# Rows of x, two modulation tables and the row statistics placed at other steps of the first two batches

## The chip, the cores and the metric

The kernel runs on one core of a Trainium2 chip. Its engines are TensorE (PE in the profile, with its weight loads as PEld), VectorE (DVE), ScalarE (ACT), GpSimd (POOL) and SyncE (SP, which here only issues transfers). Each engine works through its own list of instructions in order and waits on semaphores for the others. Transfers run on 16 DMA engines; they are issued by SP or, for a few early ones, by POOL. The metric is device time in microseconds (us) of the core, as the median of several executions.

## The reference

An adaptive layer norm with six modulation vectors, an S4D convolution (a long convolution whose kernel is a sum of 256 damped oscillations for each channel), and a token-mixing MLP:

```python
mod = (_silu(c) @ w_mod).reshape(c.shape[0], 6, 1, -1)
sa, ca, ga, sb, cb, gb = (mod[:, 0], mod[:, 1], mod[:, 2], mod[:, 3], mod[:, 4], mod[:, 5])
h = _layernorm(x, axis=-1) * (1 + ca) + sa
x = x + ga * _A_ref(h, A_log_A_real, A_A_imag, A_C_real, A_C_imag, A_log_dt, A_D_skip)
h = _layernorm(x, axis=-1) * (1 + cb) + sb
x = x + gb * _B_ref(h, B_w1, B_b1, B_w2, B_b2)
```

```python
# _A_ref
A = -jnp.exp(log_A_real) + 1j * A_imag
C = (C_real + 1j * C_imag) * dt[:, None]
P = jnp.exp((A * dt[:, None])[:, :, None] * pos[None, None, :])
K = 2.0 * jnp.einsum("dn,dnl->dl", C, P).real
y = jnp.fft.irfft(Uf * Kf[None, :, :], L2)[:, :, :L]      # Uf, Kf: rfft of u and K
# _B_ref
h = _layernorm(x, axis=-1)
u = _gelu(jnp.einsum("bsd,sf->bdf", h, w1) + b1)
y = jnp.einsum("bdf,fs->bds", u, w2) + b2
```

There are 2048 tokens, 448 channels, 256 oscillations for a channel and 1792 hidden units. Everything is float32. `shift` in this document is `sa`, the vector `mod[0]`; `mod[1]` is the scale and `mod[2]` the gate of the convolution.

## The kernel before

The program has two parts. The first, up to about 384 us, builds the convolution kernel of all channels, transforms x and the kernel, multiplies and transforms back. The second, from there to the end, is the MLP on PE. The change lies in the first 130 us of the first part.

**Steps, batches and windows.** The 448 channels are 28 groups of 16, and each group is done in two halves of 128 oscillations: 56 steps, in batches of 8. A batch opens with `window(s)` (s = 0, 8, 16, ...), in which the exponentials of its eight steps are made, and goes on with its eight steps, in which sines and cosines are made; so ACT changes its table of functions twice in a batch.

- `st_exponents(s)` (PE): parameter rows `lex` times the table `tab`, into `xe`, `xg`. `st_exp(s)` (ACT): their exponentials `mag`. `st_mag2(s)` (POOL, L654 and L656): a product `m` of them.
- `st_phase(s)` (PE): rows `lph` times `tab`, into `xe`, `xg`. `st_abs` and `st_step` (ACT, L664 to L677): sines and cosines. From these POOL makes `G` (L679, L680) and DVE makes `E` (L681 to L687), which PE multiplies in `st_kgen` (L710) two steps later. `E` and `G` have three buffers each.
- `st_s1` (PE, L748) is the first transform of the finished kernel of two groups, on alternate steps from step 8 on; its results are copied by ACT, or in the last step of a batch by DVE (L755).

**The path of x.** x stands in `xt` as 16 rows of 128 x 448 (a row here is one position r of every 16 tokens). `x_load(r0, n, G)` issues the transfers of n rows as four transfers on POOL's queue. `u_stats(r)` (DVE, L527 and L528) takes mean and variance of a row. At the start of window 8 `logs(True)` on ACT and `u_scale` on DVE turn all 16 pairs into `rs` and `nm`, so that none of it starts before the last row's statistics are there; `u_norm` (POOL for rows 0 to 5, ACT later, L543 and L541) normalises. `u_rows(r)` (PE, L553) transforms a row into two `pu` tiles, DVE multiplies these by `mod[1]` into `yt` (L556), and SP stores `yt`. Rows 0 to 4 and 5 go in window 8, one row in each of the steps 9 to 14, the last four in window 16. The tables `late_rows` (step to rows) and, in window 0, the line for rows 0 to 3 say where the statistics are taken; `between()`, which runs behind E's four operations in the steps up to 15, takes them and then goes on with the parameters of the next channels (`more`, L399 to L450).

**Modulation vectors.** `wm_load(k, place)` loads the 448 x 448 block of `w_mod` for vector k (784 KB). `modulation(k, halves)` (PE, L489) multiplies it in two halves into one `pm` tile, which ACT copies to `mod[k]` (L493) at the next `flush(act)`. `mod_steps` says in which steps; vector 0 has its two halves at e = 2 and e = 4 of window 8. In step 9 DVE multiplies `mod[0]` by `mod[2]` (L1103). `mod[0]` is first read in batch 24. The dictionary `late` says in which step each block is issued and to where; blocks 0 and 2 go to free room and on POOL's queue, block 1 to free room on SP's, block 3 over rows 0 to 3 of `xt`, which have been transformed by then.

**Queues and buffers.** The order on PE, ACT, DVE and POOL is that of the code. SP's is that of the code up to step 7; from step 8 on it is set by the scheduler. `pu`, `pm` and the results of `st_s1` share three PSUM buffers (`pms`, tag `ms`); a `pu` pair takes two.

Of the kernel before, what the change touches and what calls it, by code (L numbers as in the profile page):

```python
# [221 lines left out]
def tile_adaln_s4d_mixer(ctx, tc, i, out):  # L222
    nc = tc.nc
# [20 lines left out]
    with ExitStack() as es:  # L244
# [47 lines left out]
        PP = 112  # L292
# [35 lines left out]
        def wm_load(k, tile, eng=nc.sync):  # L328
            wms[k] = tile
            eng.dma_start(wms[k], i["w_mod"][:, k * D : (k + 1) * D].rearrange("(q p) d -> p q d", p=PP))  # L330
# [11 lines left out]
        def wm_slot(k):  # L342
            w = wm0.rearrange("p k d -> p (k d)")[0:PP]
            return w[:, 4 * D * (k % 4) : 4 * D * (k % 4 + 1)].rearrange("p (q d) -> p q d", q=4)
# [2 lines left out]

        late = {
            2: lambda: wm_load(2, wm_slot(2), G),
            3: lambda: wm_load(0, wm_slot(0), G),  # L350
            6: lambda: [
                nc.sync.dma_start(wu, i["WU"]),
                nc.sync.dma_start(wc, i["WC"].rearrange("p (c m) -> p c m", c=2)),
            ],
            9: lambda: [nc.sync.dma_start(svt, i["SV"]), wm_load(3, xt[0:PP, 0:4])],
            10: lambda: [s2_load(0), s2_load(1)],
            11: lambda: [s2_load(2), s2_load(3)],
        }


# [204 lines left out]
        def s2_load(n):  # L565
            s2s[n] = sp2.tile([P, 2, P], F32, tag="s2", name="s2", bufs=4)
            nc.sync.dma_start(s2s[n], s2_v[:, 2 * n : 2 * n + 2])
# [290 lines left out]
        def first_chain():  # L858
# [7 lines left out]
            def split(eng, src):  # L866

                hl = room.pop()
                eng.tensor_copy(hl[:, 0].bitcast(F32R), src)
                eng.tensor_tensor(hl[:, 1].bitcast(F32R), src, hl[:, 0], ALU.subtract)  # L870
                return hl
# [66 lines left out]
            tt(xa, xa, u, ALU.subtract)  # L938
            store(ha, (0, 1), (1, 1))
            hl = split(G, p64)  # L940
            direct(hl, lph, 64, 0)
            hc = split(V, xa)
            direct(hc, lph, 96, 0)
# [59 lines left out]
        def window(s):  # L1003
            angle()
            logs(s == 8)
            if s == 8:
                u_scale()
                u_norm(0)
                u_norm(1)

            if s == 0:
                st_exponents(s)
            for e in range(BATCH):
                st_exp(s + e)

                if e + 1 < BATCH:
                    st_exponents(s + e + 1)
                else:
                    st_phase(s)
                mellow()  # L1020
                if s == 8 and e == 0:
                    tt(mod[1], mod[1], mod[2], ALU.mult)
                flush(dve)
                flush(act)
                flush(late_act)
                if s < 32:
                    more(WPACE[s // 8][e])
                if s == 0 and e >= 4:
                    u_stats(e - 4)
                if s and e < (2 if s <= 32 else 1):  # L1030
                    st_kgen(s - (2 if s <= 32 else 1) + e)
                elif e == (7 if s == 32 else 5):
                    if s == 8:
                        yks[0] = y0.tile([P, 32, DC], F32, tag="yk", name="yk0")
                    st_s1(s > 16)

                if s == 8 and e in (2, 4):
                    modulation(0, e // 4)
                if s in (8, 16):
                    some(u_rows, rows, (1, 1, 1, 1, 1, 0, 0, 1)[e])  # L1040
                elif s == 24 and e != 5:
                    some(u_cols, cols, 1)

                if s == 32 and e == 2:
                    nc.sync.dma_start(t0, i["T0"].rearrange("p (j m) -> p j m", j=2))
                if s == 32 and e == 5:
                    pc_load(1)
                if s >= 40 and e == 2:
                    piece(False)
                if s >= 32 and e == 4:  # L1050
                    piece(pieces[0] < NP, V)
                if s == 0 and e in (4, 5):
                    st_mag2(e - 4)
                elif s and (e < 2 or s >= 32):
                    st_mag2(s + e)
                if s == 8 and e == 0:
                    u_norm(e + 2)
                if s == 0 and e == 3:
                    for r in range(4):
                        dsk_copy(r)  # L1060
            if s == 0:

                S.activation(one, one, AF.Sin)
# [2 lines left out]

        WPACE = [[0] * 8, [0, 2, 3, 4, 5, 5, 5, 5], [0, 5, 4, 4, 4, 4, 4, 4], [2] * 8]
        pace = [2] * 32
        mod_steps = {2: (1, 0), 3: (1, 1), 6: (2, 0, 1)}
        late_rows = {3: (4, 5), 4: (6, 7), 5: (8, 9), 6: (10, 11), 7: (12, 13, 14, 15)}  # L1070
        tail = NHALF + 3
        for s in range(tail):
            if s == 32:
# [25 lines left out]

            def between():  # L1100
                flush(dve)
                if s == 9:
                    tt(mod[0], mod[0], mod[2], ALU.mult)  # L1103
                for r in late_rows.get(s, ()):
                    u_stats(r)
                if s < len(pace):
                    more(pace[s])
# [36 lines left out]
                st_kgen(s - 1)  # L1144


            if s < 2:
                x_load(4 + 4 * s, 4 + 4 * s, G)
            free = s > 7 and not st_s1(s % BATCH == BATCH - 1)
            if s + 2 < 32 and (s + 2) % BATCH > 1:  # L1150
                st_mag2(s + 2)
# [324 lines left out]
```

## Time and profile before

| | us |
|---|---|
| median of 3 executions | 690.65 |
| these executions | 687.97, 690.65, 694.99 |
| the profiled execution, its own time | 685.43 |
| its span in the profile | 683.7 |

The rest of the profiled execution's time, 1.73 us, lies outside the span.

| engine | busy us | share of the span |
|---|---|---|
| PE | 612.7 | 90% |
| DVE | 452.6 | 66% |
| ACT | 439.0 | 64% |
| POOL | 268.1 | 39% |

These shares are means over two very different parts. From about 384 us on PE is busy nearly all the time and all else waits for it. Before that PE, DVE, ACT and POOL take turns, and what a change there is worth has to be read from the timeline of that place. A row of the timeline gives start, duration, engine, source line, operation, the tiles written and read, how many instructions are merged (a matmul of float32 shows as several), and in square brackets how long the engine had been idle and what ended that. POOL's queue carries 8 transfers of 224 KB and 4 of 448 KB for x and 2 of 784 KB for `w_mod` in this profile.

### The profile page before, as it was taken

The page shows a single profiled execution, that of the slowest core. Times are in us where ns is not written, and L with a number is a line of the kernel's source. Part 1 is how long each engine was busy: PE and PEld are TensorE (multiplying, and loading weights), DVE is VectorE, ACT ScalarE, POOL GpSimd, SP SyncE. Part 2 cuts the span into 40 slices and gives each one's busy share as a digit, 9 for nine tenths or more (in the row PEclk, how much of TensorE's full clock was granted, in tenths as well). Part 3 has the DMA queues.
Part 4 walks back from the last instruction along what each step waited for, and adds up shares of the span by engine and source line. Part 5 has one row for each costly group of instructions (what it writes and reads, how often), then busy time and mean ns, then how long its engine had stood idle before and what let it go on. Part 6 is the DMA issues. An engine that isn't in the chain of part 4 may idle for free. (4 is left out here: it accounts for less than half of the span.)

```text
span 683.7 us, 18263 instructions
## 1 busy us (share of the span) xinstructions
PE 612.7 (90%) x7180; PEld 456.0 (67%) x7180; DVE 452.6 (66%) x870; ACT 439.0 (64%) x880; POOL 268.1 (39%) x323
## 2 busy tenths in 40 slices
PE   0786778879989899989989899999999999999997
PEld 0443345535535556565657677779999999999996
DVE  7498799888779596895967587777422454433331
ACT  5967597988988999999945588877322322222220
POOL 6397457448458889789847100000000000000000
PEclk9989888999999999999999999999999999999999
DMA  7695563377896857344359799956674355555530
GB/s 176 199 201 111 181 200 120 128 269 223 251 310 190 234 116 216 97 133 136 97 140 315 237 256 255 239 128 199 160 221 135 95 142 168 165 161 170 167 119 28
DMA packets 105923, 121.14 MB, mean 177 GB/s; under 512 B 13098, under 2 KB 94286, under 8 KB 105710
## 3 DMA queue, kind: packets, MB, share of 16 engines
q1 hardware_dynamic: 104478, 113.92, 58.1%
q0 software_dynamic: 1360, 6.06, 4.1%
q8 instruction: 57, 0.93, 0.6%
q14 instruction: 28, 0.23, 0.1%
HBM read 84.59 MB, written 34.87 MB: 175 GB/s over the span
## 5 line engine op out<-in xcount | busy, mean ns | idle before, releaser
L207 ACT CAST whi<-w 128x896 fp32r<-128x896 f32 x64 | 59.8, 940 | 132.2 <-PE o L1443 84.5
L679 POOL TENSOR_TENSOR G<-mag,gs 128x512 f32<-128x512 f32 x56 | 71.8, 1281 | 66.1 <-ACT gs L675 65.9
L216 DVE TENSOR_TENSOR wlo<-w,whi 128x896 fp32r<-128x896 f32 x64 | 68.0, 1086 | 40.3 <-ACT whi L207 27.9
L1373 PE MATMUL acc<-h3h,whi 128*128 128x448 f32 x224 | 83.3, 372 | 1.6 <-ACT h3h L1278 1.6
L1374 PE MATMUL acc<-h3l,whi 128*128 128x448 f32 x224 | 82.1, 367 | 0.1
L1443 PE MATMUL o<-ul,whi 128*128 128x448 f32 x224 | 81.3, 363 | 0.0
L1375 PE MATMUL acc<-h3h,wlo 128*128 128x448 f32 x224 | 81.2, 362 | 0.0
L1442 PE MATMUL o<-uh,whi 128*128 128x448 f32 x224 | 81.2, 362 | 0.0
L1444 PE MATMUL o<-uh,wlo 128*128 128x448 f32 x224 | 80.6, 360 | 0.0
L710 PEld LDWEIGHTS kg<-E,G 128*32 128x32 f32 x3584 | 57.3, 116 | 34.9 <-issue 14.5
L627 PE MATMUL xg<-tab,lph 64*128 64x512 f32 x112 | 62.9, 563 | 12.4 <-DVE E L687 4.7
L710 PE MATMUL kg<-E,G 128*32 128x64 f32 x3584 | 67.1, 230 | 7.0 <-issue 3.3
L680 POOL TENSOR_TENSOR G<-mag,gs 128x512 f32<-128x512 f32 x56 | 71.8, 1282 | 0.0
L627 PE MATMUL xe<-tab,lph 64*128 64x512 f32 x112 | 63.5, 569 | 4.7 <-ACT gs L676 2.6
L1446 DVE SCALAR_TENSOR_TENSOR y<-o,b,mod 128x448 f32<-128x448 f32 x16 | 10.9, 684 | 80.2 <-PE o L1444 80.2
L656 POOL TENSOR_TENSOR m<-mag,w 128x512 f32<-128x512 f32 x56 | 58.9, 1052 | 4.4
L681 DVE TENSOR_TENSOR E<-m,xe 128x512 f32<-128x512 f32 x56 | 38.1, 681 | 23.2 <-ACT xe L674 19.8
L1373 PEld LDWEIGHTS acc<-h3h,whi 128*128 128x128 f32 x224 | 42.4, 189 | 14.6 <-ACT h L1283 5.6
L627 PE MATMUL xe<-tab,lex 64*128 64x512 f32 x56 | 30.9, 569 | 19.2 <-DMA lex<-wm 17.0
L1375 PEld LDWEIGHTS acc<-h3h,wlo 128*128 128x128 f32 x224 | 42.3, 189 | 3.0
L1442 PEld LDWEIGHTS o<-uh,whi 128*128 128x128 f32 x224 | 42.0, 188 | 3.4
L1374 PEld LDWEIGHTS acc<-h3l,whi 128*128 128x128 f32 x224 | 42.4, 190 | 2.7 <-DVE h3l L1281 0.5
(239 smaller groups left out, 1440.1 us busy)
## 6 DMA issues: line engine op xcount, KB each, us to landing
w<-in_B_w_dram SPq DMA_DIRECT2D x64, 224.0 KB
w<-in_B_w_dram SPq DMA_DIRECT2D x32, 448.0 KB
yu_d<-yt SPq DMA_DIRECT2D x16, 448.0 KB
yi<-yu_d SPq DMA_DIRECT2D x16, 448.0 KB
us_d<-uo SPq DMA_DIRECT2D x16, 448.0 KB
u<-us_d SPq DMA_DIRECT2D x32, 224.0 KB
v_d<-vt SPq DMA_DIRECT2D x32, 224.0 KB
vt<-v_d SPq DMA_DIRECT2D x14, 448.0 KB
```

The source lines that it names most:

```text
L207: self.nc.scalar.copy(hi, w)
L216: eng.tensor_tensor(lo, w, hi.bitcast(F32), ALU.subtract)
L627: T.matmul(out[k], lhs[r], rhs[r], start=start, stop=stop)
L679: G.tensor_tensor(Gt[:, 1], mg_, v32(sg), ALU.mult)
L680: G.tensor_tensor(Gt[:, 0], mg_, v32(cg_), ALU.mult)
L710: T.matmul(kgs[g][32 * q : 32 * q + 32, m], Gt[:, c, d], E[:, c, d], start=h == 0 and c == 0 and m == 0, stop=h == 1 and c == 1, skip_grou ...
L1373: nc.tensor.matmul(acc[f], hi[:, fs], h3h[:, r], start=r == 0, stop=False)
L1374: nc.tensor.matmul(acc[f], hi[:, fs], h3l[:, r], start=False, stop=False)
L1375: nc.tensor.matmul(acc[f], lo[:, fs], h3h[:, r], start=False, stop=r == 15)
L1442: nc.tensor.matmul(o, hi[:, ks], uh[kh][:, k], start=kh == 0 and k == 0, stop=False)
L1443: nc.tensor.matmul(o, hi[:, ks], ul[kh][:, k], start=False, stop=False)
L1444: nc.tensor.matmul(o, lo[:, ks], uh[kh][:, k], start=False, stop=kh == 1 and k == 6)
```

## The change

```diff
         late = {
             2: lambda: wm_load(2, wm_slot(2), G),
-            3: lambda: wm_load(0, wm_slot(0), G),
             6: lambda: [
...
-            9: lambda: [nc.sync.dma_start(svt, i["SV"]), wm_load(3, xt[0:PP, 0:4])],
+            9: lambda: [nc.sync.dma_start(svt, i["SV"]), wm_load(0, xt[0:PP, 0:4])],
             10: lambda: [s2_load(0), s2_load(1)],
             11: lambda: [s2_load(2), s2_load(3)],
+            12: lambda: wm_load(3, xt[0:PP, 4:8]),
         }
...
             hl = split(G, p64)
+            x_load(4, 4, G)
             direct(hl, lph, 64, 0)
...
-                if s == 8 and e in (2, 4):
-                    modulation(0, e // 4)
...
-        mod_steps = {2: (1, 0), 3: (1, 1), 6: (2, 0, 1)}
-        late_rows = {3: (4, 5), 4: (6, 7), 5: (8, 9), 6: (10, 11), 7: (12, 13, 14, 15)}
+        mod_steps = {2: (1, 0), 3: (1, 1), 6: (2, 0, 1), 12: (0, 0), 13: (0, 1)}
+        late_rows = {0: (4, 5), 3: (6, 7), 5: (8, 9, 10), 6: (11, 12, 13), 7: (14, 15)}
...
-                if s == 9:
+                if s == 15:
                     tt(mod[0], mod[0], mod[2], ALU.mult)
...
-            if s < 2:
-                x_load(4 + 4 * s, 4 + 4 * s, G)
+            if s == 0:
+                x_load(8, 8, G)
```

Rows 4 to 7 of x are issued among the first parameters, before window 0, instead of behind step 0; rows 8 to 15 behind step 0 instead of behind step 1. The block of `w_mod` for vector 0 is no longer loaded by POOL in step 3 but by SP from step 9 on, over rows 0 to 3 of `xt`; the block for vector 3 goes over rows 4 to 7, from step 12 on. The two halves of modulation 0 move from window 8 to the ends of the steps 12 and 13, its copy by ACT with them, and the product with `mod[2]` from step 9 to step 15. The statistics of the rows 4 and 5 move from step 3 to step 0, 6 and 7 from 4 to 3, 10 from 6 to 5, 12 and 13 from 7 to 6. No arithmetic is added or left out.

POOL's list, from behind the split of the first parameters to step 2, before (`xt` rows of 1792 elements are the four transfers of rows 4 to 7, those of 3584 the rows 8 to 15, L654 and L656 are `st_mag2`):

```order
L477 COPY dsk<-dskr 1x112 x4
L654 TENSOR_TENSOR w<-mag 128x16
L656 TENSOR_TENSOR m_325<-mag,w 128x512
L654 TENSOR_TENSOR w<-mag 128x16
L656 TENSOR_TENSOR m_339<-mag,w 128x512
L679 TENSOR_TENSOR G<-mag,gs 128x512
L680 TENSOR_TENSOR G<-mag,gs 128x512
L305 DMA xt<-in_A_u_dram 32x1792 x4
L654 TENSOR_TENSOR w<-mag 128x16
L656 TENSOR_TENSOR m_415<-mag,w 128x512
L679 TENSOR_TENSOR G<-mag,gs 128x512
L680 TENSOR_TENSOR G<-mag,gs 128x512
```

and now:

```order
L305 DMA xt<-in_A_u_dram 32x1792 x4
L477 COPY dsk<-dskr 1x112 x4
L654 TENSOR_TENSOR w<-mag 128x16
L656 TENSOR_TENSOR m_329<-mag,w 128x512
L654 TENSOR_TENSOR w<-mag 128x16
L656 TENSOR_TENSOR m_343<-mag,w 128x512
L679 TENSOR_TENSOR G<-mag,gs 128x512
L680 TENSOR_TENSOR G<-mag,gs 128x512
L305 DMA xt<-in_A_u_dram 32x3584 x4
L654 TENSOR_TENSOR w<-mag 128x16
L656 TENSOR_TENSOR m_425<-mag,w 128x512
L679 TENSOR_TENSOR G<-mag,gs 128x512
```

Four issues have moved from between step 0 and step 1 to ahead of window 0; the four of rows 8 to 15 stand in their old place, and nothing stands behind step 1 in theirs.

DVE's list in step 0, before (`E`, then two operations on the next parameters):

```order
L681 TENSOR_TENSOR E<-m_325,xe 128x16x32
L682 SCALAR_TENSOR_TENSOR E<-mag,xe 128x16x32
L686 TENSOR_TENSOR E<-mag,xg 128x16x32
L687 TENSOR_TENSOR E<-m_325,xg 128x16x32
L399 SCALAR_TENSOR_TENSOR s<-xa,ya 128x256
L401 TENSOR_TENSOR ya<-ya,xa 128x256
```

and now:

```order
L681 TENSOR_TENSOR E<-m_329,xe 128x16x32
L682 SCALAR_TENSOR_TENSOR E<-mag,xe 128x16x32
L686 TENSOR_TENSOR E<-mag,xg 128x16x32
L687 TENSOR_TENSOR E<-m_329,xg 128x16x32
L527 BN_STATS st<-xt 128x6
L528 BN_AGGR mv<-st 128x2
L527 BN_STATS st<-xt 128x6
L528 BN_AGGR mv<-st 128x2
L399 SCALAR_TENSOR_TENSOR s<-xa,ya 128x256
L401 TENSOR_TENSOR ya<-ya,xa 128x256
```

The statistics of rows 4 and 5 now stand between E of step 0 and the parameters; step 7 has two rows behind E where it had four.

PE's list at the end of step 12, the last two matmuls of `st_phase(13)`, the row's transform and step 13's `st_kgen`, before:

```order
L627 MATMUL xe<-tab,lph_143 128x512
L627 MATMUL xg<-tab,lph_143 128x512
L553 MATMUL pu<-xt,wu 128x448 x2
L710 MATMUL kg<-E,G 32x64 x32
L627 MATMUL xe<-tab,lph_144 128x512
```

and now:

```order
L627 MATMUL xe<-tab,lph_143 128x512
L627 MATMUL xg<-tab,lph_143 128x512
L489 MATMUL pm<-xt,scb 128x448 x2
L553 MATMUL pu<-xt,wu 128x448 x2
L710 MATMUL kg<-E,G 32x64 x32
L627 MATMUL xe<-tab,lph_144 128x512
```

Half of modulation 0 stands ahead of the row's transform, and so ahead of all that PE does behind it; the same holds one step later for the other half.

## The prediction

> **What bounds the kernel now.** I read the chain of work that ended last, then the busy times by stretch, then the timeline of each engine up to 150 us. The chain is printed only back to about 384 us, where the MLP begins; from there on PE is the bound and the change touches nothing. First its line by engine, then three stretches, for which each engine's busy time, the granted clock of PE, the DMA engines' busy share and GB/s are given: steps 0 to 2 of batch 1, window 8, and the steps 8 to 15:
>
> ```profile
> PE 42%; ACT 1%; DVE 1%; issue 0%; ACTq 0%
> ...
> core 0: us, PE busy (x) PEld busy (x) DVE busy (x) ACT busy (x) POOL busy (x), PEclk, DMA share, GB/s
> 29.50:45.00 15.50, 11.55 (x158) 6.48 (x159) 15.13 (x18) 11.02 (x23) 14.74 (x20) 0.78 0.92 204
> ...
> 71.50:92.60 21.10, 18.80 (x252) 10.46 (x252) 16.04 (x40) 14.40 (x28) 7.18 (x10) 0.88 0.67 231
> 92.60:127.30 34.70, 27.68 (x531) 17.20 (x523) 34.30 (x54) 31.01 (x61) 28.52 (x28) 0.85 0.35 121
> ```
>
> The first is carried by DVE (15.13 of 15.50) and POOL (14.74) with the DMA engines nearly full (0.92), window 8 by PE (18.80 of 21.10), steps 8 to 15 by DVE (34.30 of 34.70). The end of batch 1 is read from DVE's timeline, with the two engines that wait for it behind:
>
> ```profile
> 41.83 3.44 DVE L410 SCALAR_TENSOR_TENSOR s<-t,s 128x256 f32<-128x256 f32 x1
> ...
> 47.59 0.61 DVE L527 BATCH_NORM_STATS2 st<-xt 128x6 f32<-128x448 f32 x1
> ...
> 49.07 0.69 DVE L681 TENSOR_TENSOR E<-m,xe 128x512 f32<-128x512 f32 x1
> ...
> 57.75 0.63 DVE L527 BATCH_NORM_STATS2 st<-xt 128x6 f32<-128x448 f32 x1 [1.60 <-DMA xt<-in_A_u_dram]
> ...
> 69.55 0.18 DVE L528 BATCH_NORM_AGGREGATE mv<-st 128x2 f32<-128x6 f32 x1
> ```
>
> ```profile
> 69.77 0.31 ACT L462 ACTIVATE rs<-mv,small_t 128x16 f32<-128x16 f32 x1 [2.36 <-DVE mv L528]
> ...
> 71.47 3.10 POOL L543 TENSOR_SCALAR xt<-xt,rs,nm 128x448 f32<-128x448 f32 x4 [7.35 <-DVE nm L536]
> ```
>
> DVE ends batch 1 with the last statistics; ACT has waited 2.36 us for them and POOL 7.35 us. Between 45.27 (the end of L410) and 69.73 DVE pauses once, 1.60 us, for rows 8 and 9 of x. So batch 1 is as long as DVE's list.
>
> **Part by part, batch 1.** POOL's rows:
>
> ```profile
> 30.01 1.28 POOL L679 TENSOR_TENSOR G<-mag,gs 128x512 f32<-128x512 f32 x1 [8.49 <-ACT gs L675]
> ...
> 32.46 2.00 POOL L305 DMA_DIRECT2D xt<-in_A_u_dram  x4
> ...
> 43.70 1.28 POOL L680 TENSOR_TENSOR G<-mag,gs 128x512 f32<-128x512 f32 x1
> ...
> 46.44 0.74 POOL L330 DMA_DIRECT2D wm<-in_w_mod_dram  x1
> ```
>
> ```profile
> DMA to landing us min/median/max: 3.9/10.0/17.9
> ```
>
> 1. *Rows 8 to 15.* The issue stands where that of rows 4 to 7 stood, 32.46 to 34.46. The slowest of the x transfers landed after 17.9 us, so they are there by 52.4. DVE asks for row 8 where E of step 5 ended, 57.75 - 1.60 = 56.15, less what it gains before (2.3 us, terms 2 and 3): 53.8. The wait goes: -1.60, with 1.4 us to spare; 784 KB of block 0 and the rows 4 to 7 have also left that stretch. Ends: 0 and -1.60.
>
> 2. *Statistics.* A pair takes 49.07 - 47.59 = 1.48. Steps 3 to 7 had six pairs and have five: -1.48. The pair in step 0 falls on a busy DVE (15.13 of 15.50) and pushes everything up to L410 back by 1.48.
>
> 3. *L410.* It took 3.44, and ended 0.3 after POOL's pair L679, L680 of step 2 (43.70 + 1.28 = 44.98): DVE was held, not working. POOL's pair comes 2.00 earlier, since four issues have left its unbroken run (they lie in its 8.49 us of idle time now); block 0's issue, 0.74, leaves it later. The two ways this can go are in these rows:
>
> ```profile
> 40.91 0.89 DVE L408 TENSOR_SCALAR t<-s 128x256 f32<-128x256 f32 x1
> ...
> 107.62 1.37 DVE L410 SCALAR_TENSOR_TENSOR s<-t,s 128x256 f32<-128x256 f32 x1
> ```
>
> L408 now starts at 42.39 and is held to 42.98; with the 1.37 of the same operation in batch 2, L410 ends at about 44.4, E of step 3 starts 0.8 sooner than it did: -0.8. Ends: 45.27 - 43.7 (not held) = -1.5, and with the 3.44 again +1.2. I take the nearer row, since it stands between the same neighbours. The Trainium skill (SBUF — State Buffer, SBUF: two separate sides) says that DVE and GpSimd share a pair of SBUF ports under an exclusive lock, held for one whole instruction: a DVE operation would then be held for at most one POOL operation, 1.28 us. L408 and the second L410 agree; the 3.44 does not, as it outlasted the boundary at 43.70. By the rule the sum below stays -4.0; by the 3.44 it is -2.0.
>
> Batch 1: -1.60 - 1.48 - 0.8 = -3.9. What is late next is ACT, whose 2.36 of waiting is smaller; but ACT's sines of these steps wait for POOL's G, which comes up to 2.74 sooner (2.00 + 0.74). If ACT did not move at all, -2.36 would be left.
>
> **Window 8 and the steps behind it.**
>
> ```profile
> 77.78 1.77 PE L489 MATMUL pm<-wm,scb 112*128 112x448 f32 x4
> ...
> 82.93 1.77 PE L489 MATMUL pm<-wm,scb 112*128 112x448 f32 x4
> ...
> 114.15 0.97 PE L553 MATMUL pu<-xt,wu 64*128 64x448 f32 x4
> ...
> 117.09 1.07 PE L553 MATMUL pu<-xt,wu 64*128 64x448 f32 x4
> ...
> 120.35 1.69 PE L553 MATMUL pu<-xt,wu 64*128 64x448 f32 x4
> ```
>
> ```profile
> 80.54 1.16 DVE L556 TENSOR_TENSOR yt<-pu,mod 128x448 f32<-128x448 f32 x2 [0.47 <-PE pu L553]
> ...
> 85.68 1.15 DVE L556 TENSOR_TENSOR yt<-pu,mod 128x448 f32<-128x448 f32 x2 [0.22 <-PE pu L553]
> ...
> 98.86 1.31 DVE L1103 TENSOR_TENSOR mod<-mod,mod 128x448 f32<-128x448 f32 x1
> ...
> 116.08 1.14 DVE L556 TENSOR_TENSOR yt<-pu,mod 128x448 f32<-128x448 f32 x2
> ...
> 120.36 1.14 DVE L556 TENSOR_TENSOR yt<-pu,mod 128x448 f32<-128x448 f32 x2
> ...
> 123.81 1.14 DVE L556 TENSOR_TENSOR yt<-pu,mod 128x448 f32<-128x448 f32 x2
> ...
> 131.51 1.15 DVE L556 TENSOR_TENSOR yt<-pu,mod 128x448 f32<-128x448 f32 x2 [2.90 <-PE pu L553]
> ```
>
> 4. *Modulation 0 leaves window 8.* PE loses 2 x 1.77 = 3.54. But PE and DVE hand three PSUM buffers to and fro there, and behind the two places DVE waited for PE only 0.47 + 0.22: -0.7. Ends: 0 and -3.54.
>
> 5. *The product leaves step 9:* -1.2, DVE having no idle time there (L1103 less the 0.1 by which rows overlap). In step 15 it stands ahead of DVE's last work, and 2.90 us of waiting follow: 0. Ends: -0.6 and -2.5 (where the operations behind it meet fewer of POOL's).
>
> 6. *Modulation 0 enters steps 12 and 13,* 1.77 ahead of the `pu` of 114.15 and 1.77 ahead of that of 117.09. These ended 0.96, 2.20 and (the third) 1.77 before DVE read them. Late: 1.77 - 0.96 = 0.8, then 3.54 - 2.20 = 1.3, then 3.54 - 1.77 = 1.8. I take +1.8. Ends: 0 (PE's list starts as much sooner as DVE's) and the half-clock price below. ACT's copy changes places at equal length.
>
> 7. *Blocks 0 and 3.* SP issues block 0 where it issued block 3, and block 3 some 30 us later:
>
> ```profile
> 85.41 0.36 SPq L330 DMA_DIRECT2D xt<-in_w_mod_dram  x1
> ...
> DMA to landing us min/median/max: 16.1/17.2/18.3
> ...
> 141.98 3.27 PE L489 MATMUL pm<-xt,scb 112*128 112x448 f32 x8
> ```
>
> Block 0: 85.4 + 18.3, the longest landing of a block on POOL's queue, is 103.7, and PE reads it at 114. Block 3 is issued around the `pu` of 114.15, say at 115; 115 + 18.3 = 133, and PE reads it at 142. Both: 0. Of the parameter rows behind block 3's issue on SP's queue the first come 0.36 later, for a step that begins some us later: 0.
>
> Sum: -3.9 - 0.7 - 1.2 + 1.8 = -4.0. Behind step 15 all lists are as before and each transfer is issued behind the step that frees its buffer, so I carry the shift to the end. The profiled execution, 685.43 us, would take 681.4; it lies 5.2 below the median of the runs shown, so their median becomes 690.65 - 4.0 = 686.6.
>
> **Rivals.** *Modulation at half clock* (0.12), the one that ends slower:
>
> ```profile
> 38.71 3.22 PE L489 MATMUL pm<-wm,scb 112*128 112x448 f32 x4 [1.55 <-DMA wm<-in_w_mod_dram]
> ...
> 40.00:42.00 2.00, 2.00 (x11) 0.48 (x13) 1.97 (x4) 0.34 (x1) 1.86 (x4) 0.50 1.00 232
> ...
> 112.00:114.00 2.00, 2.00 (x27) 1.45 (x19) 2.00 (x5) 0.00 (x0) 1.92 (x3) 0.50 0.28 103
> 114.00:116.00 2.00, 2.00 (x72) 1.34 (x68) 2.00 (x4) 1.60 (x4) 0.01 (x1) 1.00 0.51 185
> ```
>
> Half a modulation took 3.22 in step 2, where the granted clock was 0.50 from 40 to 42; it was 0.50 again from 112 to 114, just ahead of the new place. With 3.22 twice, term 6 is +6.4, the sum +0.6 and the time 691.3. It decides once term 6 exceeds 5.8, that is when nearly all of both halves runs at half clock and nothing of it lies beside DVE's work. Against it: from 114 on the clock was full. The Trainium skill (TensorE: Matmul & The Clock Gate, What's actually happening) grants half rate only after an idle window of about 3.4 us and full rate after a busy one; by that rule a PE that has more to do here stays at full rate, term 6 stays at +1.8 and the sum at -4.0. The row from 112, all busy and yet at 0.50, agrees only if a pause shortly before counts as such a window.
>
> *More of it is free* (0.20): term 6 at 0, term 4 at -1.6 (PE's list bounds the window for half of what leaves it), term 5 at -2.5, batch 1 at -4.6 (L410 not held, -1.5): -8.7, 682.0. For it: PE and DVE wait for each other in these steps, so that a DVE that comes sooner by term 5 also starts PE sooner. Against: PE is busy all 4.00 us from 112 to 116, without room for 1.77.
>
> *ACT holds the end of batch 1* (0.20): -2.36 in place of -3.9, sum -2.5, 688.2. For it: 2.36 is all its slack. Against: the sines of these steps start when POOL has freed their buffers, and POOL's list is shorter by 2.74.
>
> *The early rows crowd the first parameters* (0.06):
>
> ```profile
> 16.00:20.00 4.00, 2.34 (x6) 1.12 (x6) 3.73 (x15) 1.61 (x4) 2.24 (x5) 1.00 0.28 64
> ```
>
> Four transfers of 224 KB at the 204 GB/s of the busy stretch are 4.5 us; between 16 and 20 us 0.72 x 4 = 2.9 us are free. The rest, 1.6, could delay every step: sum -2.4, 688.3.
>
> **How the numbers follow.** The forecast keeps 0.42, 686.6 (its own range 684.5 to 689). The range of 8 in 10 takes in the crowding, ACT and half-clock cases and most of the free one: 681.5 to 691.5. One per cent, 6.9 us, is about what a measurement here tells from no change, the runs shown lying 7 apart. Faster by over 1% (below 683.7) needs the free case: 0.20. Slower by over 1% needs something that I don't see: 0.05. Within 1%: 0.75.
>
> **What would show it.** No DMA in front of DVE's statistics in step 5, and ACT's L462 near 65.9. L410 near 1.4. Window 8, from L462 to E of step 8, shorter by 0.7. No product between the E's of the steps 9 and 10, and these 1.2 closer together. DVE waiting for `pu` about 1 us ahead of E in the steps 13 to 15, the L489 there at 1.77 each where the clock is full and 3.22 where it is not. The prediction is wrong if L462 comes before 65 or after 68, if the sines of window 16's first step do not come about 4 us sooner, or if what is gained there is not found again at the start of the MLP.

## The result and the profile after

| | before | after |
|---|---|---|
| median, us (20 executions each) | 689.04 | 685.31 |
| lowest to highest, us | 685.08 to 695.2 | 681.71 to 692.01 |
| ratio of the two, 95% interval | | 0.9948 (0.9926 to 0.997) |
| profiled execution, its own time | 685.43 | 685.58 |

The changed kernel is 3.6 us faster (0.0052 x 689), less than the 1% within which the prediction put it. The two profiled executions do not show it: that of before lies 3.6 below its median, that of after at its median. So a difference of the two traces is trusted only where more profiles agree; fourteen are at hand in the end.

First after's busy times in the three stretches, now from E of step 0, from L462 and from E of step 8 (columns as in the prediction):

```profile
core 0: us, PE busy (x) PEld busy (x) DVE busy (x) ACT busy (x) POOL busy (x), PEclk, DMA share, GB/s
32.94:48.44 15.50, 12.14 (x182) 6.75 (x182) 15.14 (x25) 12.86 (x27) 14.73 (x18) 0.89 0.87 192
69.80:90.90 21.10, 17.03 (x244) 9.88 (x244) 15.96 (x40) 13.95 (x27) 7.23 (x10) 0.84 0.65 222
90.90:124.00 33.10, 29.60 (x545) 16.39 (x539) 30.91 (x55) 31.60 (x63) 28.00 (x28) 0.85 0.48 156
```

The same engines carry the same stretches; the third is 1.6 shorter, and DVE (30.91 of 33.10) now has idle time there. Then DVE's timeline of batch 1 in after, and ACT's end of it:

```profile
32.96 0.69 DVE L681 TENSOR_TENSOR E<-m,xe 128x512 f32<-128x512 f32 x1 [11.46 <-ACT xe L674]
...
44.76 1.98 DVE L408 TENSOR_SCALAR t<-s 128x256 f32<-128x256 f32 x1
46.78 0.42 DVE L410 SCALAR_TENSOR_TENSOR s<-t,s 128x256 f32<-128x256 f32 x1
...
56.72 0.61 DVE L527 BATCH_NORM_STATS2 st<-xt 128x6 f32<-128x448 f32 x1
```

```profile
68.15 0.31 ACT L462 ACTIVATE rs<-mv,small_t 128x16 f32<-128x16 f32 x1 [2.38 <-DVE mv L528]
```

E of step 0 starts at 32.96, 3.44 later than before, but row 8 is waited for by nobody (56.72 has no bracket) and L462 comes 35.19 behind E of step 0 where it came 40.25 behind (69.77 - 29.52). The late start is PE's; first its timeline in before, then in after:

```profile
16.96 0.76 PE L627 MATMUL xe<-tab,lex 64*128 64x512 f32 x1 [16.96 <-DMA lex<-wm]
18.16 0.79 PE L627 MATMUL xg<-tab,lex 64*128 64x512 f32 x1 [0.44 <-DMA lex<-wm]
```

```profile
17.32 0.76 PE L627 MATMUL xe<-tab,lex 64*128 64x512 f32 x1 [17.32 <-DMA lex<-wm]
21.60 0.79 PE L627 MATMUL xg<-tab,lex 64*128 64x512 f32 x1 [3.52 <-DMA lex<-wm]
```

The second matmul waits 3.52 for a piece of `lex` (32 KB) that SP has issued, while POOL issues four transfers of 224 KB from 15.47 on. Last, the modulation in its new place in after:

```profile
108.74 1.77 PE L489 MATMUL pm<-xt,scb 112*128 112x448 f32 x4
...
113.67 1.77 PE L489 MATMUL pm<-xt,scb 112*128 112x448 f32 x4
```

```profile
111.50 1.15 DVE L556 TENSOR_TENSOR yt<-pu,mod 128x448 f32<-128x448 f32 x2 [0.59 <-PE pu L553]
...
116.42 1.15 DVE L556 TENSOR_TENSOR yt<-pu,mod 128x448 f32<-128x448 f32 x2 [1.20 <-PE pu L553]
```

Both halves run at full clock and DVE waits 0.59 + 1.20 behind them. From here on places are told by the start of a step's first sine on ACT (L674). Step 16 starts 4.61 earlier in after; at step 32 that is gone in these two traces (237.07 before, 236.98 after), which the experiments take up.

### The profile page after: what moved, and what is told of

Its sections match the earlier page's. It is cut to its first block, busy times and chain, and to the rows that moved or that the text cites. A ratio compares the mean times of both kernels' runs of the same rounds, so it can differ in the third digit from the quotient of the medians.

```text
span 683.7 us, 18268 instructions
## 1 busy us (share of the span) xinstructions
PE 614.2 (90%) x7180; PEld 455.9 (67%) x7180; DVE 446.5 (65%) x870; ACT 438.8 (64%) x880; POOL 267.6 (39%) x322
## 5 line engine op out<-in xcount | busy, mean ns | idle before, releaser
L679 POOL TENSOR_TENSOR G<-mag,gs 128x512 f32<-128x512 f32 x56 | 72.1, 1288 | 66.9 <-ACT gs L675 66.7
L680 POOL TENSOR_TENSOR G<-mag,gs 128x512 f32<-128x512 f32 x56 | 71.8, 1281 | 0.0
L656 POOL TENSOR_TENSOR m<-mag,w 128x512 f32<-128x512 f32 x56 | 59.7, 1065 | 4.4
L681 DVE TENSOR_TENSOR E<-m,xe 128x512 f32<-128x512 f32 x56 | 38.2, 682 | 26.0 <-ACT xe L674 21.9
L638 ACT ACTIVATE mag<-xe 128x512 f32<-128x512 f32 x56 | 35.5, 635 | 13.9 <-PE xe L627 5.7
```

Of the source, the lines that this page charges most:

```text
L679: G.tensor_tensor(Gt[:, 1], mg_, v32(sg), ALU.mult)
L680: G.tensor_tensor(Gt[:, 0], mg_, v32(cg_), ALU.mult)
```

## The experiments

### Rows 4 to 7 issued later

```diff
             hl = split(G, p64)
-            x_load(4, 4, G)
...
                     st_mag2(e - 4)
+                    if e == 5:
+                        x_load(4, 4, G)
...
-        late_rows = {0: (4, 5), 3: (6, 7), 5: (8, 9, 10), 6: (11, 12, 13), 7: (14, 15)}
+        late_rows = {1: (4, 5), 3: (6, 7), 5: (8, 9, 10), 6: (11, 12, 13), 7: (14, 15)}
```

> The changed kernel with one transfer moved: the four issues of rows 4 to 7 stand on POOL's list behind the second pair of st_mag2 of window 0 (about 21.5 us) and no longer ahead of the window; the statistics of rows 4 and 5 move from step 0 to step 1, so that they don't wait for them. Theory (these transfers delay the second piece of lex, and all steps start 3.44 us late): the first sine of step 0 comes back from 32.26 to 28.8, batch 1 stays about 5 us shorter than before, and the time is 3.4 below the changed kernel's, 7.0 below that of before (ratio 0.990). First rival (the late start has another cause, such as the place of the memory reads of lex): the start stays near 32 and the time at the changed kernel's, ratio 0.995. Second rival (whatever is gained early is given back at window 32, as in the profiled execution of the changed kernel): the start comes back, but from step 32 on the steps start as in before, ratio 0.995 to 1.000.

Measured: 693.86, ratio 1.0084 (1.0051 to 1.0118), so this kernel is slower than before. The four issues stand at 21.81 here. The start came back, to 29.74, so the early issues are what delayed it. But PE in step 2 of this kernel then had a new wait:

```profile
48.83 3.35 PE L489 MATMUL pm<-wm,scb 112*128 112x448 f32 x4 [8.24 <-DMA wm<-in_w_mod_dram]
```

SP had issued block 1 at 32.51, POOL the rows 8 to 15 (1.8 MB) from 33.39 on. Step 4 started at 56.02, 9.5 later than in before. None of the three expectations had this.

### Early rows alone

```diff
             hl = split(G, p64)
+            x_load(4, 4, G)
...
-            if s < 2:
-                x_load(4 + 4 * s, 4 + 4 * s, G)
+            if s == 1:
+                x_load(8, 8, G)
```

> The kernel before with rows 4 to 7 issued where the changed kernel issues them, and nothing else (rows 8 to 15 stay behind step 1, statistics and modulation as before). Theory (crowding): the first sine of step 0 at about 32.3, +3.44; POOL has four issues less behind step 0, so L410 is held somewhat less, -0.8 to -1.5; the wait for rows 8 and 9 goes too if they are still issued near 38, since DVE comes later, down to -1.6. The time lies 0.5 to 2.7 above before, ratio 1.001 to 1.004. Rival (the steps of batch 1 absorb a late start because POOL and not DVE carries them): ratio 1.000 or below, with step 8 starting no later than 91.9.

Measured: 689.16, ratio 1.0013 (0.9996 to 1.003). Start 31.40 with a wait of 2.35 for `lex`, no wait for rows 8 and 9, step 8 at 91.16. The early rows cost at the start about what they bring later. The delay is smaller than expected, and the interval holds the ratios of the theory and of its rival. The rival's sign is there: step 8 starts before 91.9, and of the 2.3 by which the start is later than in before (29.08 in the mean of four profiles) 0.6 is left at step 4 (47.35 against 46.76), as POOL has no issue behind step 0 any more.

### Transfers and statistics

The edit above, with `if s == 0: x_load(8, 8, G)` and the changed kernel's `late_rows`.

> The kernel before with the early rows, rows 8 to 15 behind step 0 and the statistics of the changed kernel; modulation 0, its block and its product stay in window 8 and step 9. Theory (the two parts add): start +3.44, batch 1 about 5 shorter, step 8 about 1.7 earlier than before and 1.7 still at step 16; block 0, 784 KB, is again issued in step 3 and may hold POOL by its 0.74. Ratio 0.9975, 1.7 below before. Rival (all of the gain of the changed kernel is in batch 1): ratio 0.995, as the changed kernel. Second rival (block 0 in step 3 brings the wait for x back): step 8 as in before, ratio 1.000.

Measured: 687.45, ratio 0.9996 (0.9981 to 1.0012). Batch 1 is short (L462 35.41 behind the first sine), but the start is at 33.75, with 4.29 of waiting for `lex`: about nothing is left. The expected 1.7 lies just outside the interval. The ratio is that of the second rival, but its cause is not there: no statistics wait for x in this profile.

### Modulation alone

```diff
-            3: lambda: wm_load(0, wm_slot(0), G),
...
-            9: lambda: [nc.sync.dma_start(svt, i["SV"]), wm_load(3, xt[0:PP, 0:4])],
+            9: lambda: [nc.sync.dma_start(svt, i["SV"]), wm_load(0, xt[0:PP, 0:4])],
...
+            12: lambda: wm_load(3, xt[0:PP, 4:8]),
...
-                if s == 8 and e in (2, 4):
-                    modulation(0, e // 4)
...
-        mod_steps = {2: (1, 0), 3: (1, 1), 6: (2, 0, 1)}
+        mod_steps = {2: (1, 0), 3: (1, 1), 6: (2, 0, 1), 12: (0, 0), 13: (0, 1)}
...
-                if s == 9:
+                if s == 15:
```

> The kernel before with the part on modulation alone: block 0 loaded by SP from step 9 on, block 3 from step 12, the halves of modulation 0 in steps 12 and 13, the product in step 15. Theory (read from the two traces: between the starts of step 8 and step 16 the changed kernel gains 2.9): step 8 starts as in before or up to 1 earlier (POOL has no block to issue in step 3), step 16 about 2.9 earlier, ratio 0.996. Rival (the prediction's terms 4 to 6: -0.7, -1.2 and +1.8): ratio 1.000. Second rival (the gain between the steps 8 and 16 hangs on the earlier rows): ratio 1.000, with waits for PE in the steps 13 to 15 larger than the product that left.

Measured: 686.81, ratio 0.998 (0.9957 to 1.0002). Step 16 starts at 141.39, 3.7 before that of the first profile. The steps 8 to 16 take 51.24, 1.95 less than in the first profile, where 2.9 was expected; so a gain is there without the earlier rows. What of it the median shows, 1.4, is not told apart from either end.

### Rows 8 to 15 behind block 1

The first experiment with `if s == 1` in place of `if s == 0` at `x_load(8, 8, G)`.

> As the first run (rows 4 to 7 behind the second pair of st_mag2, statistics of rows 4 and 5 in step 1), with rows 8 to 15 issued behind step 1 as in before, so that block 1 of w_mod, issued by SP at about 32, is ahead of them. In the first run PE waited 8.24 for this block at 48.83. Theory (1.8 MB of rows on the DMA engines at once made block 1 late, nothing else): the wait is below 2, step 4 starts at about 46.5, step 8 at 88 (3.9 before that of the kernel before), step 16 about 7 earlier, ratio 0.991. Rival (the sum of the transfers is what counts, 4.2 MB up to 45 us, wherever they stand): block 1 or rows 8 and 9 are waited for by 3 or more, step 8 not before 91, ratio 0.996 or above.

Measured: 683.04, ratio 0.9911 (0.9879 to 0.9943). PE's L489 of step 2 starts at 40.15 without a wait, L462 comes at 66.69, step 8 at 88.27. The rival falls: it is where the transfers stand that counts. Step 16 starts at 140.26, 4.8 earlier than in the first profile of before and not 7; of the missing 2.2, step 15 to 16 accounts for 1.3 (22.21 against 20.89 in after).

### Modulation and spread statistics, old transfers

The modulation run with `late_rows = {2: (4, 5), 3: (6, 7), 5: (8, 9, 10), 6: (11, 12, 13), 7: (14, 15)}`.

> The run on modulation alone with the statistics spread as far as the old transfers allow: rows 4 and 5 in step 2, 6 and 7 in 3, 8 to 10 in 5, 11 to 13 in 6, 14 and 15 in 7; rows 4 to 7 issued behind step 0, 8 to 15 behind step 1. No transfer stands ahead of the first parameters. Theory (a pair less in steps 3 to 7, 1.48, and no crowding): start 28.8 to 29.3, step 8 about 3.2 and step 16 about 5.2 earlier than in before, ratio 0.994. Rival (DVE, now earlier, waits for row 8 or rows 4 and 5 by what it gains): step 8 about 1.8 earlier as in the run on modulation alone, ratio 0.998.

Measured: 686.52, ratio 0.9956 (0.9928 to 0.9984). The rival's wait is there, on DVE of this kernel, and larger than the pair that was saved:

```profile
46.41 0.63 DVE L527 BATCH_NORM_STATS2 st<-xt 128x6 f32<-128x448 f32 x1 [5.32 <-DMA xt<-in_A_u_dram]
```

Step 8 starts at 91.62, where the mean of four profiles of before is 91.59. So statistics can be spread this far only with rows that are issued earlier. The ratio lies between the two that were expected, and its interval takes in both.

### The last two blocks apart

```diff
-            if s in (34, 36):
-                late_load(s // 2 - 13)
+            if s in (36, 44):
+                late_load(4 + s // 44)
```

This edit was made in the changed kernel, in before, and in the version with the rows 8 to 15 behind block 1. The trace of after had shown, between steps 31 and 33, PE held under "issue" while the DMA engines were full, and then half clock:

```profile
229.14 0.50 PE L627 MATMUL xe<-tab,lex 64*128 64x512 f32 x1 [2.97 <-issue]
```

```profile
226.00:230.00 4.00, 1.03 (x8) 0.53 (x8) 0.17 (x1) 2.28 (x5) 3.70 (x6) 1.00 1.05 212
230.00:234.00 4.00, 3.69 (x18) 1.70 (x14) 1.89 (x4) 2.83 (x6) 2.80 (x5) 0.51 1.07 211
```

> The changed kernel with the two last blocks of w_mod (L503, 784 KB each) asked for in the steps 36 and 44 and not 34 and 36; SP's list now has the first of them behind the u rows of window 32 and the second behind that window's lex pieces. In the changed kernel's trace the DMA engines were full (1.05 to 1.07) from 226 to 234, PE waited 2.97 under issue, and step 31 to 32 took 18.14 where it had taken 14.67 before. Theory (the two blocks close together fill the DMA engines and hold PE's instructions and its lists): step 31 to 32 takes 15 or less, the DMA share from 230 to 234 is below 0.9, the time 3 below the changed kernel's, ratio 0.990. Rival (that loss is of the one profiled execution, and the blocks cost nothing in the median): ratio 0.995.

> The kernel before with only the two last blocks of w_mod moved to the steps 36 and 44. Theory (in most executions the DMA engines are full from 226 to 234 and cost PE 3 to 4 us; the first profile of before, with 18.1 from step 31 to 33, was an exception, the second with 22.3 the rule): step 31 to 33 takes 19.6 or less, ratio 0.9965. Rival (the blocks are not what costs): step 31 to 33 takes 20 or more, ratio 1.000.

> The run with rows 4 to 7 behind the second st_mag2 and rows 8 to 15 behind step 1, and with the two last blocks of w_mod in the steps 36 and 44. Theory (the parts add): step 31 to 33 as in the run with the blocks apart, 19.6 or less, start near 30, ratio 0.989 (681.5 to 682.5 against 689.5). Rival (at window 32 the blocks' place only matters where the transfers happen to collide, as the earlier run without it had 18.6 there): no difference from that run, ratio 0.991.

Measured: 683.97, ratio 0.9932 (0.9902 to 0.9962) in the changed kernel; 689.32, ratio 0.9998 (0.9974 to 1.0023) in before; 682.56, ratio 0.9917 (0.9885 to 0.9949) in the third, whose ratio without it had been 0.9911. Step 31 to 33 took 19.59, 18.58 and 21.68 with the edit and 18.11 to 22.31 without it, so that single profiles decide nothing here. In the changed kernel's profile the DMA share from 230 to 234 did fall, to 0.60, and step 31 to 32 took 16.15. But no median shows the 2 to 3 us that the blocks were to cost: before with the edit is at 0.9998, and each of the other two is within 0.0016 of its ratio without it. The theory falls; a smaller gain, in before of up to 1.8 us by the interval, can't be excluded.

### Before, a second time

> The kernel before, profiled a second time. Its first profile lay 3.6 below its median, and its step 31 to 32 took 14.67; in the five other profiles so far it took 15.28 to 18.14. Theory (the first profile was a lucky one, and what the changed kernel seemed to lose at window 32 is lost by the kernel before as well in most executions): 15.3 to 18.1 here, start of step 0 near 28.8 and step 16 near 145.1 as in the first profile. Rival (the earlier lists of the changed kernels cause the loss): 14.7 again.

Measured: 689.2. Step 31 to 33 took 22.31, against 18.11 in the first profile; the start (29.16) is alike, and step 16 starts at 143.85. The granted clock at that place in this profile (the first had 1.00 in all rows):

```profile
230.00:234.00 4.00, 2.30 (x14) 1.18 (x13) 0.85 (x2) 2.47 (x6) 3.77 (x7) 0.90 1.08 257
234.00:238.00 4.00, 3.70 (x50) 2.28 (x52) 1.06 (x3) 3.13 (x7) 3.17 (x5) 0.50 1.04 253
238.00:242.00 4.00, 4.00 (x50) 2.95 (x45) 3.01 (x6) 3.51 (x7) 1.73 (x2) 0.50 0.26 71
```

So the kernel before loses there too in some executions: its first profile was lucky, and what after seemed to give back at window 32 is not shown to be an effect of the change. From step 16 to step 55 the fourteen profiles take 196.7 (the first of before) to 203.7 us, though no edit but that of the blocks and the next one touches the work there.

### Modulation 0 in step 16

```diff
-        mod_steps = {2: (1, 0), 3: (1, 1), 6: (2, 0, 1), 12: (0, 0), 13: (0, 1)}
+        mod_steps = {2: (1, 0), 3: (1, 1), 6: (2, 0, 1)}
...
+                        modulation(0, 0, 1)
                         modulation(3, 0, 1)
...
-                if s == 15:
+                if s == 17:
```

> The changed kernel with modulation 0 beside modulation 3 in step 16 and the product in step 17; transfers, statistics and blocks as in the changed kernel. From step 12 to 13 the kernels with modulation 0 in window 8 took 6.77 to 6.92, those with it in the steps 12 and 13 4.29. Theory (the 1.77 of modulation in step 12 fills PE's wait ahead of the row's transform, and so the clock stays full): step 12 to 13 takes 6.8 again, the DVE waits for pu in steps 13 to 15 are gone, step 16 starts 1 to 2.5 later than in the changed kernel, and step 16 carries 3.5 more of PE: ratio 0.998 to 1.002. Rival (the product that left step 9 lets DVE, and with it PE, come earlier, and the modulation only costs): step 12 to 13 takes 4.3, steps 13 to 16 are shorter by the 1.8 of waits for pu, ratio 0.993 to 0.995.

Measured: 683.79, ratio 0.9916 (0.9882 to 0.995). Step 12 to 13 takes 4.28: the theory of the modulation as a filler falls. The rival's second sign is missing too: the steps 13 to 16 took 30.27, where the changed kernel took 29.22 and 30.25 (with the blocks apart), as PE stood still for 2.69 at 114.21 (last section). That this place is better than steps 12 and 13 is not settled, as the intervals overlap.

### The product alone

```diff
-                if s == 9:
+                if s == 15:
                     tt(mod[0], mod[0], mod[2], ALU.mult)
```

> The kernel before with one edit: the product of mod[0] and mod[2] in step 15 and no longer in step 9. Theory (modulation as filler): steps 9 to 10 shorter by up to 1.2, step 12 to 13 still 6.8, so that PE's half-clock spell takes back most: step 16 within 0.7 of the kernel before, ratio 1.000. Rival (the product was what made PE late): step 12 to 13 takes 4.3, step 16 about 2.5 or more earlier, ratio 0.996.

Measured: 686.55, ratio 0.9956 (0.9929 to 0.9984). One line gives what the whole change gives. Step 12 to 13 takes 4.29 and the steps 8 to 16 take 49.72, where kernels with the product in step 9 took 52.9 to 53.4. DVE in this kernel, to be read against the prediction's rows of L408, L410 and L1103:

```profile
99.77 0.65 DVE L405 TENSOR_TENSOR ya<-ya,xa 128x256 f32<-128x256 f32 x1
103.79 0.47 DVE L408 TENSOR_SCALAR t<-s 128x256 f32<-128x256 f32 x1
104.29 0.43 DVE L410 SCALAR_TENSOR_TENSOR s<-t,s 128x256 f32<-128x256 f32 x1
```

and POOL beside it:

```profile
103.06 1.05 POOL L656 TENSOR_TENSOR m<-mag,w 128x512 f32<-128x512 f32 x1
105.33 1.29 POOL L679 TENSOR_TENSOR G<-mag,gs 128x512 f32<-128x512 f32 x1 [1.22 <-ACT gs L675]
```

L408 and L410 were 1.30 and 1.37 long and are 0.47 and 0.43: they now end at 104.72, and L410 lies in a pause of POOL, which is done with L656 at 104.11 and waits for ACT until 105.33. In before they lay from 106.28 on, beside L679 and L680 (106.16 to 108.70). What that did to PE, and PE to ACT, stands in these rows of before:

```profile
109.58 1.02 PE L553 MATMUL pu<-xt,wu 64*128 64x448 f32 x2 [1.52 <-ACT gs L675]
```

```profile
114.40 0.60 ACT L664 ACTIVATE ab<-xe 128x512 f32<-128x512 f32 x1 [2.51 <-PE xg L627]
```

The second half of a row's transform needs a `pu` buffer that DVE's L556 (108.91 on) frees. The profile puts the wait down to an ACT instruction that ended at the same moment; in two other profiles with the product in step 9 it names L556 for the same wait, and in all five of them PE starts 0.06 after L556 has ended. The product alone has no such wait. PE's busy time and clock, first before, then the product alone, then the kernel before with the blocks apart:

```profile
108.00:112.00 4.00, 2.48 (x59) 1.77 (x62) 4.00 (x7) 3.89 (x8) 3.92 (x5) 0.82 0.22 82
112.00:116.00 4.00, 4.00 (x95) 2.79 (x85) 4.00 (x8) 1.60 (x4) 1.94 (x3) 0.75 0.40 144
```

```profile
108.00:112.00 4.00, 3.93 (x83) 2.53 (x80) 4.00 (x9) 4.00 (x9) 3.84 (x6) 1.00 0.46 162
112.00:116.00 4.00, 3.40 (x83) 2.26 (x80) 4.00 (x9) 4.00 (x10) 3.92 (x5) 1.00 0.39 135
```

```profile
108.00:112.00 4.00, 2.47 (x69) 1.21 (x66) 3.97 (x7) 4.00 (x8) 3.92 (x6) 1.00 0.10 37
112.00:116.00 4.00, 3.56 (x93) 2.32 (x81) 4.00 (x8) 2.30 (x5) 2.50 (x4) 1.00 0.39 145
```

In before PE has run dry behind a late DVE (2.48 of 4.00 busy), its granted clock is down (0.82, then 0.75), and ACT waits for it (1.60 busy). With DVE early PE has no gap there, keeps its clock, and the wait is gone. The third kernel tells the two apart by chance: it has the product in step 9 and the same wait of PE (1.53), but full clock here. Its step 12 to 13 takes 6.11, against 6.92 at the lower clock and 4.29 without the wait. So by this one profile PE's wait for DVE is worth about 1.8 of the 2.6 and the clock 0.8; over the steps 8 to 16 that kernel is no faster (53.44).

## Why the prediction came out right

The forecast was 4.0 less than a median of 690.65, that is 686.6; measured were 685.31 and a gain of 3.6 against a median of 689.04. Yet two terms were wrong by 3.4 and 2.3 us, with opposite signs, so that the closeness of the sum is luck. In this table the measured values are means over profiles with the same list up to that place: of before four (two of the kernel itself, the product alone, the blocks alone; for the last row the three with the product in step 9), of after three (itself, the blocks apart, modulation in 16; for the last row the first two).

| place | before | after | difference | predicted |
|---|---|---|---|---|
| first sine of step 0 | 29.08 | 32.51 | +3.43 | 0 |
| from there to L462 | 39.86 | 35.81 | -4.05 | -3.9 |
| L462 to the first sine of step 8 | 22.65 | 22.41 | -0.24 | -0.7 |
| step 8 to 16 | 53.17 | 50.62 | -2.55 | +0.6 |
| sum | | | -3.41 | -4.0 |

1. *Rows 8 to 15:* right in kind. No statistics wait for a transfer. The wait itself was 1.60 and 1.00 in the two profiles of before and 1.26 in the mean of the four with its list. From E of step 5 to L462, where of the first three terms only this one is left, the gain is 1.3 and not 1.6.

2. *Statistics:* right, -1.48. The run of transfers and statistics has a pair less ahead of E of step 5 than the run of the early rows alone; it comes there 21.57 after the first sine, the other 23.09.

3. *L410 held less:* the gain is there, but not for the reason given. L408 and L410 together fall from 4.33 to 2.40; it is L408 that is held now, from 44.76 to 46.74, while POOL works off L679 (44.08 to 45.36) and L680 (to 46.58). So the hold outlasts a boundary of POOL's again; in the run of the early rows alone it was 3.06. The Trainium skill (SBUF — State Buffer, SBUF: two separate sides) states a lock that is held for one whole instruction. That DVE gets the ports at POOL's next boundary was the prediction's own step from there, and these rows speak against it.

   The step that failed is "batch 1 is as long as DVE's list", which counts the held time of DVE as work. A profile with before's list, that of the blocks alone, has L410 by chance not held, and DVE then waits for ACT:

```profile
42.16 0.43 DVE L410 SCALAR_TENSOR_TENSOR s<-t,s 128x256 f32<-128x256 f32 x1
...
45.80 0.69 DVE L686 TENSOR_TENSOR E<-mag,xg 128x512 f32<-128x512 f32 x1 [2.02 <-ACT xg L677]
```

   L410 is 2.9 to 3.0 shorter there, and yet E of step 5 comes 24.70 after the first sine, against 24.73 to 24.85 in the three profiles where it was held. What sets these steps is POOL's list, through ACT, whose L675 waits for a `gs` buffer that POOL's L679 frees; first before, then after:

```profile
43.79 0.60 ACT L675 ACTIVATE gs<-xg 128x512 f32<-128x512 f32 x1 [3.46 <-POOL G L679]
```

```profile
45.40 0.60 ACT L675 ACTIVATE gs<-xg 128x512 f32<-128x512 f32 x1 [1.62 <-POOL G L679]
```

   The wait is shorter by nearly the 2.00 of the four issues that left POOL's list. Priced so, the term is -1.7 and not -0.8: E of step 5 comes 23.09 after the first sine in the run of the early rows alone, which changes no statistics. Block 0's issue gives 0.7 by the run on modulation alone (24.10), but nothing on top of the rest in the changed kernel (21.99). The sum of the three terms, -3.9, measured -4.05 because two errors cancel: up to E of step 5 the gain is 2.8 in place of 2.3, and behind it 1.3 in place of 1.6.

4. *Modulation 0 leaves window 8:* too large. L462 to step 8 varies by 1.9 between profiles of like lists, and the mean gain is 0.2, which is not told apart from the lower end, 0.

5. *The product:* mis-sized, -1.2 where the run of the product alone shows 49.72 - 53.17 = -3.5. The step that failed is "less the 0.1 by which rows overlap": only L1103's own time was counted. From E of step 9 to E of step 12 that run takes 13.86 (95.36 to 109.22), the first profile of before 17.45 (96.24 to 113.69), 3.6 more: 1.2 of product, and 2.2 of L405, L408 and L410 (0.40, 0.83 and 0.94 shorter), which no longer meet POOL as they did. The end of -2.5 named this and was still short.

6. *Modulation enters 12 and 13:* +1.8 predicted; the changed kernel's 50.62 less the product's 49.72 leaves +0.9, and the run on modulation alone +1.5. These are single profiles, and the kernel with modulation 0 in step 16 takes 50.93 without it, so the size stays open. The half-clock rival didn't come: 1.77 at full clock.

7. *Blocks 0 and 3:* nothing was seen to wait for them, as predicted.

*Crowding,* given 0.06 and 1.6, happened in every kernel that had the early issues: waits for `lex` of 2.35 to 4.29, the start 2.1 to 5.0 later than the mean of before. The step that failed is the division of the four transfers' time over the free share of the DMA engines between 16 and 20 us. The engines had been at 0.99 from 14 to 16 us in before, and in after they stay full or nearly so to 22 us (the last three columns are PE's clock, the DMA share and GB/s):

```profile
16.00:18.00 2.00, 0.68 (x1) 0.28 (x1) 1.83 (x9) 0.00 (x0) 1.94 (x5) 1.00 1.12 273
18.00:20.00 2.00, 0.08 (x1) 0.00 (x0) 1.90 (x7) 0.60 (x1) 1.72 (x5) 1.00 0.96 205
20.00:22.00 2.00, 0.40 (x2) 0.40 (x4) 1.44 (x5) 0.00 (x0) 0.50 (x1) 1.00 0.93 176
```

Before had 0.33, 0.23 and 0.57 there. So the engines stay full for longer than the 4.5 us of the estimate, and a small piece that SP issues next to the large ones waits 2.35 to 4.29 and not for a surplus of 1.6. That the issues cause it is shown by the three kernels with the issue at 21.8 to 21.9 (starts 29.50 to 30.03): in the one with the rows 8 to 15 behind block 1 the engines are full from 22 to 26 us (0.93 and 0.96), when PE is already at work on `lex` (wait 0.41). How the engines share their time between the queues was not tried.

*ACT holds the end of batch 1* did not happen (L462 still waits 2.38 for DVE); it does in the version with rows 8 to 15 behind block 1, where L462 waits for nothing. *More of it is free* was right on the product alone.

Of the prediction's own signs of being wrong one came true: L462 was to come between 65 and 68 and came at 68.15, and at 67.07 and 69.72 in the two other profiles with its list, because of the late start. The sines of window 16's first step came about 4 us sooner, as was asked for (141.03 for 144.94 in the mean of two and three profiles). Whether that is found again at the start of the MLP the traces don't decide: its first matmul comes at 393.62 and 392.01 in two profiles of the changed list and at 393.69 to 397.78 in three of before's.

So the forecast was right through a sum: +3.4 that it had as a rival, against 2.3 more from the product and 0.4 from the terms 4 and 6 together. The version with the issue at 21.9 and the rows 8 to 15 behind block 1 is nearly free of the crowding: 683.04, 6.1 below before by the ratio. That it beats the changed kernel is not shown: the intervals (0.9879 to 0.9943 and 0.9926 to 0.997) overlap, and at step 16 it and its variant with the blocks apart start at 140.26 and 140.98, the changed kernel and its variant at 140.49 and 141.56.

## What to carry to other kernels

Price a moved instruction by its neighbours too: which operations behind it shift, and whether they then meet another engine's work or its pause; here one instruction of 1.31 us was worth 3.5. DMA engines that are half idle in the mean of some microseconds do not make an early large transfer free: look which small transfer is on the path in the microseconds behind its issue, and put the large one behind it. Time in which an engine is held counts as busy in these views; look what it would have waited for without the hold before pricing it. Before explaining where a gain was lost further on, profile the old kernel a second time.

## What was not expected of the hardware

Single executions differ by fixed amounts at places that no edit touches. The steps 24 to 31 took 29.39 to 29.42 us in eleven of the fourteen profiles and 31.87 to 31.89 in three. The same four microseconds in the version with the rows 8 to 15 behind block 1 (29.41) and in its variant with the blocks apart (31.89):

```profile
200.00:204.00 4.00, 4.00 (x78) 2.27 (x77) 3.96 (x10) 2.75 (x6) 3.46 (x4) 1.00 0.81 262
```

```profile
200.00:204.00 4.00, 4.00 (x69) 1.93 (x67) 3.81 (x8) 2.42 (x5) 2.89 (x4) 0.65 0.91 302
```

PE is busy throughout in both; in the second its granted clock was 0.65, and 0.57 once more at 216 to 220. PE's longest idle time in the 10 us ahead of it was 1.48 us in both. The Trainium skill (TensorE: Matmul & The Clock Gate, What's actually happening) ties half rate to an idle window of about 3.4 us; no single pause here is that long. Either a window that is partly idle is enough, or the pauses of several microseconds add up; no run here tells these apart.

PE can also stand still under "issue", for which the profile shows no semaphore: 2.97 at 229.14 in after and 3.06 at 232.37 in the version with the blocks apart and the rows 8 to 15 behind block 1, where the DMA engines are nearly full (0.94 to 1.15 and 0.85 to 1.04 in each microsecond of the wait), and 2.69 at 114.21 in the kernel with modulation in step 16. There the share was 1.08 when the wait began and 0.22 in its last full microsecond, so full engines alone do not explain it. What PE waits for was not tried.
